# Decay attention and two MLPs on one core: one shape for the score and value matmuls, an order that counts shape changes, six P buffers

## Chip, cores and metric

One core of a Trainium2 chip runs the whole program in one launch. The metric is the device time of the launch in microseconds; lower is better.

## What is computed

Attention with a causal mask and a decay over 4 batches of 8 heads, 576 positions, 64 channels a head; its output, as 2304 tokens of 512 channels, goes through two MLPs (512 to 2048 to 512) with different activations.

```python
scores = scale * np.matmul(q, k.transpose(0, 1, 3, 2))
cum = np.cumsum(np.log(np.clip(f, 0.0001, 1.0)), axis=-1)
decay = cum[:, :, :, None] - cum[:, :, None, :]
scores = np.where(causal, -1000000000.0, scores + decay)
attn = np.exp(scores - np.max(scores, axis=-1, keepdims=True))
attn = attn / (np.sum(attn, axis=-1, keepdims=True) + 1e-09)
attn_out = np.matmul(attn, v)
...
h = x @ w_in; g = np.where(h >= 1, h, np.where(h <= -1, 0.0, (h + 1) ** 2 / 4)); x = g @ w_out
...
h = x @ w_in2; P = a0 + a1*h + a2*h2 + a3*h3; Q = 1 + abs(b0)*abs(h) + abs(b1)*h2; out = (P / (Q + 1e-6)) @ w_out2
```

## The kernel before

**Attention.** Two heads make a pair (16 pairs); head 0 lies on partitions 0 to 63, head 1 on 64 to 127. Each operand of an fp32 product is split into a high and a low part, so a product is three matmuls. A pair's queries are cut into nine blocks (`BLOCKS`): first the last 64 queries of both heads together (the block that the code calls `both`), then the blocks of 128 queries from the last to the first, each for head 0 and head 1. The tasks of a pair (`tasks_of_pair`) are, in the names that the order lists print:

- S, scores in PSUM (L414; L405 for the joint block). For a block of 128 queries the two heads run as pairs of matmuls on partitions 0 to 63 and 64 to 127, which the trace shows starting together: ql by kh, qh by kl, qh by kh, and last the decay, `one` by `ct` ("c"), which reads 2 partitions a head. So TensorE sees a tile of 64 rows three times and then one of 32 rows (2 are used). The joint block uses all 128 rows.
- M (L436, VectorE) adds the mask, takes the row's extreme and writes P; E (L448, ScalarE) is the exponential.
- T (L460) transposes P through TensorE, 128 keys at a time; the last keys are 64, so that piece fills 64 partitions. C (L473, L475, by way of `copy`, L329 on ScalarE and L331 on VectorE) copies T out of PSUM to PT.
- V (L500) multiplies PT with v into O; each head gives 64 columns, so the tile is 128 rows by 64 columns, and 64 by 64 for the last keys. R1 to R6 are the row sums' reciprocals; rT (L528) transposes them, 9 columns.

PSUM has four banks for S, two for T and two for O. `PB` is 5: P has five buffers.

**What fills TensorE beside it.** Weights come in as 64-bit words and are converted (L92 to L112, on ScalarE and VectorE), then split (L126, L130). Of the first MLP's first two chunks of 512 tokens, the products with the first four of the sixteen weight groups (h, L683, and a, L764) are spread through the attention as soon as the pairs that they need are done. After the attention come the rest of both MLPs: h (L683) and a (L777, L779).

**The order.** `plan` makes it: each task has a key (its wanted place), engines that may run it with a stated duration, tasks it needs, and buffers that it takes and frees. It goes through the ready tasks and takes the one with the least of "when it can start, by the stated durations" plus `wk` times its key:

```python
cand = (choice[1] + wk * key, key, n, choice[1], choice[2])
```

Of tasks with two engines it also picks the engine. The list so made is emitted once and then stands: on the chip every engine works through its list in order and waits at semaphores, whatever the stated durations were. The MLP part is planned by a second call.

Of the kernel before, what the change touches and what calls it, by code (L numbers as in the profile page):

```python
# [7 lines left out]
F32 = mybir.dt.float32  # L8
# [4 lines left out]
ALU = mybir.AluOpType  # L13
# [5 lines left out]
def kernel(ctx, tc, qT, kT, v, f, w_in1, w_out1, w_in2, w_out2, a, b, out):  # L19
# [24 lines left out]
    CM, CE = 80, 144  # L44
    PB = 5
    FILL = 2
    SB, TB_, OB, RB = 4, 2, 2, 2
    KM, KEX, KT, KC, KV, KR, KX, PKL, LK, FE, FS = 0.0, 1.0, 2.0, 2.0, 4.0, 2.0, 9.0, 5.0, 12.0, 170.0, 40.0
    I_K, I_Q = 4.4, 5.2
    CS = 12.0  # L50
    WARM, WARM2 = 12, 14
    WK = 0.003

# [127 lines left out]
    qd = [[ap1.tile([P, P], F32R, name=f"qd{y}{n}") for y in "hl"] for n in range(2)]  # L181
    ct = [ap1.tile([P, S], F32R, name=f"ct{n}") for n in range(2)]
    one, oned = [ap1.tile([P, P], F32R, name=f"one{x}") for x in range(2)]
    half = ap1.tile([P, 2], F32, name="half")
# [17 lines left out]
    def load_pair(pr, x):  # L202
        if x < 2:
            t = ap2.tile([P, S], F32, tag=("ks", "qs")[x], name=f"{'kq'[x]}s{pr}")
            SP.dma_start(t[:], (kT, qT)[x][pr])
        else:
            t = ap2.tile([P, NC, P], F32, tag="vn", name=f"vn{pr}")
            SP.dma_start(
                t[:, 0:NC - 1, :], v[pr, 0:(NC - 1) * P, :].rearrange("(c p) d -> p c d", p=P)
            )  # L210
            SP.dma_start(t[0:QB, NC - 1, :], v[pr, (NC - 1) * P:S, :])
        nat[pr, x] = t
# [22 lines left out]
    def task(key, eng, dur, fn, deps=(), take=(), free=()):  # L235
# [3 lines left out]
        return len(tasks) - 1  # L239

    done, by = {}, {}
    clock = dict.fromkeys(LAT, T0)
    clock["sp"] = 3.0
# [4 lines left out]
    def plan(first, wk):  # L248
# [10 lines left out]
        while ready:  # L259
            best = None  # L260
            for n in ready:
                key, ways, deps, take, _ = tasks[n]
                free_at = 0.0
                ok = True
                need = {}
                for tag in take:
                    k = need[tag] = need.get(tag, 0) + 1
                    if len(bufs[tag]) < k:
                        ok = False
                        break  # L270
                    free_at = max(free_at, sorted(bufs[tag])[k - 1])
                if not ok:
                    continue
                choice = None
                for w, (eng, dur, _) in enumerate(ways):
                    at = max(clock[eng], free_at)
                    for d in deps:
                        e2 = by[d]
                        at = max(at, done[d] + (0.13 if e2 == eng and eng != "pe" else 0.0 if e2 == eng else LAT[e2]))
                    end = at + dur if len(ways) > 1 else 0.0  # L280
                    if choice is None or end < choice[0]:
                        choice = (end, at, w)

                cand = (choice[1] + wk * key, key, n, choice[1], choice[2])
                if best is None or cand < best:
                    best = cand
# [8 lines left out]
            if eng == "sp":  # L295
                for issue, moved in dur:
                    dma[0] = max(dma[0], at) + issue
                    dma[1] = max(dma[1], dma[0] + 0.64) + MOVE * moved
                clock[eng] = dma[0]
                done[n] = dma[1] + LAND  # L300
            elif eng == "init":
                done[n] = dur
            else:
                clock[eng] = at + dur
                done[n] = at + dur
# [33 lines left out]
    def tasks_of_pair(pr):  # L339
# [48 lines left out]
        for pos, (b, j) in enumerate(BLOCKS):  # L388
# [8 lines left out]
            def s_fn(s=s, b=b, both=both, cuts=cuts):  # L397
# [13 lines left out]
                for x, (qq, kk_) in enumerate(((ql_, kh), (qh, kl_), (qh, kh), (one, c_))):  # L411
                    for jj in range(2):
                        pp = slice(jj * QB, jj * QB + (QB if x < 3 else 2))
                        PE.matmul(  # L414
                            ts[jj][:, 0:n], qq[pp, qc] if x < 3 else qq[pp, :], kk_[pp, 0:n], start=(x == 0), stop=(x == 3)
                        )
# [3 lines left out]
            if j == 1:  # L420
                tid[pr, f"S{pos}"] = tid[pr, f"S{pos - 1}"]
            else:
                dur = 4 * sum(mm(n1 - n0) for n0, n1 in cuts) if both else 4 * max(mm(w), 0.22)
                T(f"S{pos}", s, "pe", 0.08 + dur, s_fn, ("klo", "ldc", "qlo", "qd0", "qd1", prev), ("S", "S"),
                  ("k", "q") if pos == NB - 2 else ())

            def max_fn(s=s, w=w, pos=pos, both=both):
# [25 lines left out]
            for c0, c1 in [(0, LAST), (LAST, NC)] if both else [(0, b + 1)]:  # L453
                rows = QB if c0 == LAST else P

                def t_fn(s=s, c0=c0, c1=c1, rows=rows):
                    p = Pt[s]
                    ps = Tt[s, c0] = psT.tile([P, 512], F32, tag="T", name=f"T{s}_{c0}")
                    for c in range(c0, c1):
                        PE.transpose(  # L460
                            ps[0:rows, (c - c0) * P:(c - c0 + 1) * P], p[:, c * P:c * P + rows], ident[:]
                        )

                T(f"T{pos}_{c0}", s + KT, "pe", 0.107 * (c1 - c0), t_fn, (f"E{pos}",),
                  ("T",), ("P",) if c1 == b + 1 else ())

                def c_fn(eng, s=s, g=g, j=j, qo=qo, c0=c0, c1=c1, rows=rows, both=both):
                    if (pr, g) not in PT:
# [3 lines left out]
                    if both:  # L472
                        copy(eng, to[0:rows, c0:c1, :, qo:qo + QB], src[0:rows, 0:n].rearrange("p (c j x) -> p c j x", j=2, x=QB))  # L473
                    else:
                        copy(eng, to[0:rows, c0:c1, j, qo:qo + P], src[0:rows, 0:n].rearrange("p (c x) -> p c x", x=P))  # L475

# [7 lines left out]
        for g in (1, 0):  # L484
# [5 lines left out]
            for c in range(ncs):  # L490
                c_q = max(0, c * P - q0)
                rows = QB if c == LAST else P

                def pv_fn(g=g, c=c, c_q=c_q, rows=rows, n=n, ncs=ncs):
                    if c == 0:
                        Ot[pr, g] = psO.tile([P, 512], F32, tag="O", name=f"O{pr}_{g}")
                    o, pt = Ot[pr, g], PT[pr, g]
                    for j in range(2):
                        pp = slice(j * D, (j + 1) * D)
                        PE.matmul(  # L500
                            o[pp, c_q:n], nat[pr, 2][0:rows, c, pp], pt[0:rows, c, j, c_q:n],
                            start=(c == 0), stop=(c == ncs - 1),
# [3 lines left out]

                T(f"V{g}{c}", s0 + last + KV, "pe", mm(n - c_q, 4) + 0.06, pv_fn,
                  deps + ["ldv"] + ([f"V{g}{c - 1}"] if c else []) + (["V14"] if g == 0 else []), ("O",) if c == 0 else (),
                  ((f"PT{g}",) + (("v",) if g == 0 else ())) if c == ncs - 1 else ())

            def o_fn(eng, g=g, q0=q0, n=n):
# [9 lines left out]
        def r1():  # L521
            r = Rt[pr] = ap2.tile([P, NB], F32, tag="r", name=f"r{pr}")
            DVE.tensor_scalar(out=r[:], in0=ls[pr][:], scalar1=1e-9, scalar2=None, op0=ALU.add)
            DVE.reciprocal(r[:], r[:])

        def r2():
            Rr[pr] = psT.tile([P, 512], F32, tag="T", name=f"rT{pr}")
            PE.transpose(Rr[pr][0:NB, 0:P], Rt[pr][:], ident[:])  # L528

# [562 lines left out]
```

## Time and profile before

| | us |
|---|---|
| three runs | 1020.82, 1021.68, 1025.32; median 1021.68 |
| the profiled execution | 1021.83 |
| its span, first to last instruction | 1020.0 |
| TensorE (PE) busy | 1003.8 (98%) |
| VectorE (DVE), ScalarE (ACT), GpSimd (POOL) busy | 739.6, 631.9, 377.0 |

Matmul records carry modelled ends, and they overlap, so a busy PE says little of what it costs. The distance from one matmul's start to the next one's start is what a matmul takes when nothing is waited for, and it is read from the timeline.

### The profile page before, as it was taken

What the parts mean: (1) busy time and instruction counts of PE and PEld (TensorE: products, weight loads), DVE (VectorE), ACT (ScalarE), POOL (GpSimd) and SP (SyncE); (2) the same over time, 40 slices, a digit from 0 to 9 for tenths busy, and PEclk for the clock granted to TensorE, in tenths of its full rate; (3) what the DMA queues carried; (4) which work ended last, traced back from release to release, by engine and by line L of the source; (5) the groups of instructions that cost most, each with busy time, mean ns of one, the idle gap of its engine ahead of it and who ended that gap; (6) DMA issues with size and microseconds to landing.
All of it is one profiled execution on the core that took longest, in us unless ns stands there. A gap on an engine that the chain in (4) does not pass through costs nothing.

```text
span 1020.0 us, 15449 instructions
## 1 busy us (share of the span) xinstructions
PE 1003.8 (98%) x5274; PEld 796.4 (78%) x5274; DVE 739.6 (73%) x1411; ACT 631.9 (62%) x1312; POOL 377.0 (37%) x331
## 2 busy tenths in 40 slices
PE   8999999999999999999999999999999999999998
PEld 4665666666767888888888998888888888888887
DVE  6888997867287798786874577967667667657646
ACT  5787777767455443433432468876677667666666
POOL 3223320122365532222222133545454444445344
PEclk7999999999999999999999999999999999999999
DMA  5455766622456347565561454001101000010010
GB/s 187 152 176 172 220 204 204 190 67 69 158 189 227 118 152 238 161 205 166 156 225 63 131 179 125 1 10 33 42 0 42 8 35 16 6 42 1 1 42 21
DMA packets 62790, 113.13 MB, mean 111 GB/s; under 512 B 9452, under 2 KB 20348, under 8 KB 62712
## 3 DMA queue, kind: packets, MB, share of 16 engines
q1 hardware_dynamic: 62712, 112.15, 34.5%
q8 instruction: 42, 0.69, 0.3%
q14 instruction: 36, 0.29, 0.1%
HBM read 82.00 MB, written 30.11 MB: 110 GB/s over the span
## 4 chain that ended last, share of the span: by engine, by line
PE 89%; DVE 4%; ACT 2%; issue 2%; DMA 1%; POOL 1%; SPq 1%; ACTq 0%; DVEq 0%
PE h L683 35%; PE a L779 18%; PE a L777 16%; PE S L414 6%; PE T L460 5%; PE O L500 5%; PE a L764 2%; PE S L405 1%; DVE xl L672 1%; POOL wl L130 1%; ACT P L448 0%; DMA xr<-xd 0%; ACT PT L329 0%; DMA qs<-in_q_dram 0%; PE rT L528 0%
## 5 line engine op out<-in xcount | busy, mean ns | idle before, releaser
L697 POOL TENSOR_TENSOR gl<-t,gh 128x512 fp32r<-128x512 f32 (+1 forms) x160 | 195.7, 1224 | 323.3 <-ACT gh L693 238.9
L683 PE MATMUL h<-xl,wh 128*128 128x512 f32 (+1 forms) x640 | 236.5, 370 | 2.4 <-DVE xl L672 2.1
L683 PE MATMUL h<-xh,wl 128*128 128x512 f32 (+1 forms) x640 | 237.2, 371 | 1.0 <-ACT xh L668 1.0
L683 PE MATMUL h<-xh,wh 128*128 128x512 f32 (+1 forms) x640 | 235.6, 368 | 0.0
L693 ACT CAST gh<-t 128x512 fp32r<-128x512 f32 (+1 forms) x160 | 93.0, 582 | 112.7 <-PE a L779 47.8
L728 POOL TENSOR_TENSOR t<-t,t 128x512 f32<-128x512 f32 (+1 forms) x80 | 94.5, 1181 | 126.8 <-ACT t L721 123.4
L683 PEld LDWEIGHTS h<-xl,wh 128*128 128x128 f32 x640 | 120.7, 189 | 25.1 <-DVE xl L672 5.8
L683 PEld LDWEIGHTS h<-xh,wl 128*128 128x128 f32 x640 | 120.7, 189 | 22.3 <-ACT xh L668 1.4
L683 PEld LDWEIGHTS h<-xh,wh 128*128 128x128 f32 x640 | 120.7, 189 | 19.9
L779 PE MATMUL a<-wh,gl 128*128 128x512 f32 x288 | 112.3, 390 | 0.0
L779 PE MATMUL a<-wl,gh 128*128 128x512 f32 x288 | 112.2, 390 | 0.0
L779 PE MATMUL a<-wh,gh 128*128 128x512 f32 x288 | 112.1, 389 | 0.0
L777 PE MATMUL a<-gl,wh 128*128 128x512 f32 (+1 forms) x288 | 105.3, 366 | 0.0
L777 PE MATMUL a<-gh,wl 128*128 128x512 f32 (+1 forms) x288 | 105.3, 366 | 0.0
L777 PE MATMUL a<-gh,wh 128*128 128x512 f32 (+1 forms) x288 | 105.3, 365 | 0.0
L707 ACT ACTIVATE t<-t 128x512 f32<-128x512 f32 (+1 forms) x80 | 47.1, 589 | 91.6 <-DVE t L702 91.3
L746 DVE SCALAR_TENSOR_TENSOR t<-t,na,h 128x512 f32<-128x512 f32 (+1 forms) x80 | 55.4, 692 | 57.2 <-ACT h L742 56.1
L448 ACT ACTIVATE P<-P,nm 128x576 f32<-128x576 f32 (+2 forms) x144 | 83.7, 584 | 19.1 <-DVE nm L436 16.9
L702 DVE TENSOR_SCALAR t<-h 128x512 f32<-128x512 f32 (+1 forms) x80 | 50.7, 633 | 58.5 <-PE h L683 58.4
L732 DVE TENSOR_TENSOR t<-h,t 128x512 f32<-128x512 f32 (+1 forms) x80 | 51.0, 637 | 48.8 <-ACT t L724 48.5
L436 DVE CUSTOM_DVE_ANT_0 P<-S,tri 128x256 f32<-128x256 f32 (+1 forms) x144 | 66.9, 477 | 17.1 <-PE S L414 15.8
L718 ACT ACTIVATE t<-h,ab 128x512 f32<-128x512 f32 (+1 forms) x80 | 51.9, 651 | 41.9 <-PE h L683 41.7
(115 smaller groups left out, 1905.5 us busy)
## 6 DMA issues: line engine op xcount, KB each, us to landing
raw<-in_moe_w_in_dram SPq DMA_DIRECT2D x32, 512.0 KB
raw<-in_moe_w_out_dram SPq DMA_DIRECT2D x32, 512.0 KB
xr<-xd SPq DMA_DIRECT2D x48, 256.0 KB
wfd<-wd SPq DMA_DIRECT2D x44, 256.0 KB
wf<-wfd SPq DMA_DIRECT2D x44, 256.0 KB
ks<-in_k_dram SPq DMA_DIRECT2D x16, 288.0 KB
qs<-in_q_dram SPq DMA_DIRECT2D x16, 288.0 KB
xd<-xa SPq DMA_DIRECT2D x16, 288.0 KB
```

What stands on the lines that cost most here:

```text
L414: PE.matmul(ts[jj][:, 0:n], qq[pp, qc] if x < 3 else qq[pp, :], kk_[pp, 0:n], start=(x == 0), stop=(x == 3))
L436: DVE.tensor_tensor_reduce(out=p[:, n0:n1], in0=t[:, 0:n1 - n0], in1=m, scale=-1.0 / ROOT, scalar=least, op0=ALU.add, op1=ALU.min, accum_o ...
L448: ACT.activation(p, p, AF.Exp, scale=-1.0, bias=nm[pr][:, pos:pos + 1], accum_out=ls[pr][:, COL[pos]:COL[pos] + 1])
L460: PE.transpose(ps[0:rows, (c - c0) * P:(c - c0 + 1) * P], p[:, c * P:c * P + rows], ident[:])
L683: PE.matmul(hps[g], ww[:, kk * P:(kk + 1) * P], xx[kk], start=(kk == 0 and y == 0), stop=(kk == KD - 1 and y == 2))
L693: ACT.copy(gt[g][0], mid[g][0])
L697: eng.tensor_tensor(out=lo, in0=mid.pop(g)[0], in1=hi.bitcast(F32), op=ALU.subtract)
L718: ACT.activation(mid[g]["w"], hps[g], AF.Abs, scale=ab[:, 0:1])
L728: POOL.tensor_tensor(out=vv, in0=vv, in1=mid[g]["w"], op=ALU.add)
L746: DVE.scalar_tensor_tensor(out=t, in0=t, scalar=na[:, 0:1], in1=hps[g], op0=ALU.add, op1=ALU.mult)
L777: PE.matmul(acc[x, d], ww[:, dd], gg, start=st, stop=sp)
L779: PE.matmul(acc[x, d], gg[:, dd], ww[:], start=st, stop=sp)
```

## The change

Four things are changed together.

1. c's matmul reads 64 partitions a head (`ct` and `one` were zero and one there already), so all four matmul pairs of S have a tile of 64 rows by 128 columns.
2. The last keys are handled as a full piece of 128: T takes keys 448 to 575, v's last piece lies on partitions 64 to 127 of a tile whose first 64 are zero (`vt`, two tiles made once, set to zero by GpSimd at the start), and V's last product has 128 rows. rT transposes 128 columns (`rt_`) where it had 9.
3. `plan` keeps the last shape at TensorE. S tasks carry "rows", V tasks "columns", all others none. A TensorE task of another shape than the last gets `SWC` added when candidates are compared, and `SWT` to its duration. The keys' offsets `KT`, `KC`, `KV` grow (T, C and V are wanted two or three blocks later), `WK` grows, loads lead by more (`LK`, `PKL`), and the stated durations of S and V are changed.
4. P has six buffers.

```diff
-    PB = 5
+    PB = 6
-    KM, KEX, KT, KC, KV, KR, KX, PKL, LK, FE, FS = 0.0, 1.0, 2.0, 2.0, 4.0, 2.0, 9.0, 5.0, 12.0, 170.0, 40.0
+    KM, KEX, KT, KC, KV, KR, KX, PKL, LK, FE, FS = 0.0, 1.0, 4.0, 4.0, 7.0, 2.0, 9.0, 7.0, 14.0, 170.0, 40.0
-    WK = 0.003
+    WK = 0.025
+    SWC, SWT = 0.1, 0.19
...
+    vt = [ap1.tile([P, NC, P], F32, name=f"vt{n}") for n in range(2)]
+    rt_ = [ap1.tile([P, P], F32, name=f"rt{n}") for n in range(2)]
+    for n in range(2):
+        POOL.memset(vt[n][0:QB, NC - 1, :], 0.0)
+        POOL.memset(rt_[n][:], 0.0)
...
-            SP.dma_start(t[0:QB, NC - 1, :], v[pr, (NC - 1) * P:S, :])
+            SP.dma_start(t[QB:P, NC - 1, :], v[pr, (NC - 1) * P:S, :])
...
-                cand = (choice[1] + wk * key, key, n, choice[1], choice[2])
+                turn = SWC if ways[0][0] == "pe" and shape.get(n) != at_shape[0] else 0.0
+                cand = (choice[1] + turn + wk * key, key, n, choice[1], choice[2])
...
+                if eng == "pe" and shape.get(n) != at_shape[0]:
+                    at_shape[0] = shape.get(n)
+                    dur += SWT
...
-                        pp = slice(jj * QB, jj * QB + (QB if x < 3 else 2))
+                        pp = slice(jj * QB, (jj + 1) * QB)
...
-                dur = 4 * sum(mm(n1 - n0) for n0, n1 in cuts) if both else 4 * max(mm(w), 0.22)
-                T(f"S{pos}", s, "pe", 0.08 + dur, s_fn, ("klo", "ldc", "qlo", "qd0", "qd1", prev), ("S", "S"),
+                dur = 4 * sum(mm(n1 - n0) for n0, n1 in cuts) if both else 4 * max(mm(w), 0.12)
+                T(f"S{pos}", s, "pe", 0.02 + dur, s_fn, ("klo", "ldc", "qlo", "qd0", "qd1", prev), ("S", "S"),
...
+                if not both:
+                    shape[tid[pr, f"S{pos}"]] = "rows"
...
-                        PE.transpose(
-                            ps[0:rows, (c - c0) * P:(c - c0 + 1) * P], p[:, c * P:c * P + rows], ident[:]
-                        )
+                        k0 = min(c * P, S - P)
+                        PE.transpose(ps[:, (c - c0) * P:(c - c0 + 1) * P], p[:, k0:k0 + P], ident[:])
...
-                            o[pp, c_q:n], nat[pr, 2][0:rows, c, pp], pt[0:rows, c, j, c_q:n],
+                            o[pp, c_q:n], nat[pr, 2][:, c, pp], pt[:, c, j, c_q:n],
...
-                T(f"V{g}{c}", s0 + last + KV, "pe", mm(n - c_q, 4) + 0.06, pv_fn,
+                T(f"V{g}{c}", s0 + last + KV, "pe", mm(n - c_q, 4) + 0.03, pv_fn,
...
+                shape[tid[pr, f"V{g}{c}"]] = "columns"
...
-            PE.transpose(Rr[pr][0:NB, 0:P], Rt[pr][:], ident[:])
+            PE.transpose(Rr[pr][:, 0:P], rt_[pr % 2][:], ident[:])
```

New lines move the numbers: what was L414, L460, L500, L528, L436, L331 is L430, L478, L515, L544, L454, L347.

**TensorE's list in the third pair (pr = 2), before**, from the end of the 512-wide S to the start of the 384-wide one. S_0_618 and S_0_619 are the two heads; O_0 is the product for the first 256 queries; T_4 is the last keys.

```order
L414 MATMUL S_0_618<-ct_127,one_129 128x512
L414 MATMUL S_0_619<-ct_127,one_129 128x512
L528 MATMUL rT_631<-ident,r_601 9x128
L460 MATMUL T_0_633<-ident,P_596 128x128 x4
L500 MATMUL O_0_647<-PT_0_582,vn_179 64x256 x2
L460 MATMUL T_4_654<-ident,P_596 64x128
L500 MATMUL O_0_647<-PT_0_582,vn_179 64x128 x2
L414 MATMUL S_0_661<-kh_115,ql_120 128x384
```

**The same pair in the change**, from the end of the 256-wide S to the start of the 128-wide one.

```order
L430 MATMUL S_0_651<-ct_127,one_137 128x256
L430 MATMUL S_0_652<-ct_127,one_137 128x256
L478 MATMUL T_4_664<-ident,P_574 128x128
L478 MATMUL T_0_666<-ident,P_597 128x128 x4
L515 MATMUL O_0_674<-PT_0_570,vt_130 64x256 x2
L515 MATMUL O_0_674<-PT_0_570,vt_130 64x128 x2
L478 MATMUL T_0_688<-ident,P_604 128x128 x4
L478 MATMUL T_0_698<-ident,P_661 128x128 x3
L430 MATMUL S_0_704<-kh_115,ql_120 128x128
```

The two pieces of O_0 now stand side by side with no transposition between, the transpositions of three blocks stand around them, and the 256-wide S follows the 384-wide one directly.

**VectorE's list in that pair, before**, from the maximum of the first 512-wide block (the rows with nm alone read out its result).

```order
L436 ISA P_638,nm_594<-S_0_618,tri 128x512
L436 ISA nm_594 128x1
L331 COPY PT_1_650<-T_0_633 128x8x64
L436 ISA P_659,nm_594<-S_0_619,tri 128x512
L436 ISA nm_594 128x1
L96 TENSOR_SCALAR wd<-wd 128x512
L100 TENSOR_SCALAR wd<-wd 128x512
L436 ISA P_696,nm_594<-S_0_661,tri 128x384
```

**And in the change.**

```order
L454 ISA P_597,nm_572<-S_0_560,tri 128x512
L454 ISA nm_572 128x1
L347 COPY PT_0_570<-T_0_581 128x128
L454 ISA P_604,nm_572<-S_0_561,tri 128x512
L454 ISA nm_572 128x1
L382 TENSOR_TENSOR ql_122<-qs_268,qh_121 128x576
L385 TENSOR_TENSOR qdl_126<-ql_122,half 128x128
L347 COPY xa_624<-O_1_593 128x320
```

The 512-wide copy of the joint block's T has left VectorE here (ScalarE has it now), a 128-wide one of the pair before stands in its place, and a copy of O has come to it.

## Rows read from the trace of the kernel before

**Rows 1.** The page: span, and busy time of each engine.
```profile
span 1020.0 us, 15449 instructions
PE 1003.8 (98%) x5274; PEld 796.4 (78%) x5274; DVE 739.6 (73%) x1411; ACT 631.9 (62%) x1312; POOL 377.0 (37%) x331
```

**Rows 2.** Windows: busy us by engine in five stretches, TensorE's granted clock, DMA.
```profile
core 0: us, PE busy (x) PEld busy (x) DVE busy (x) ACT busy (x) POOL busy (x), PEclk, DMA share, GB/s
12.00:30.00 18.00, 17.61 (x76) 10.46 (x76) 11.65 (x38) 10.57 (x31) 1.66 (x2) 0.55 0.44 145
30.00:90.00 60.00, 56.92 (x423) 36.56 (x421) 53.00 (x161) 48.27 (x138) 19.19 (x15) 0.97 0.53 163
90.00:140.00 50.00, 48.80 (x337) 33.27 (x336) 47.83 (x121) 37.75 (x102) 15.98 (x14) 1.00 0.66 202
140.00:260.00 120.00, 120.00 (x841) 81.41 (x841) 88.76 (x261) 85.80 (x243) 20.86 (x20) 1.00 0.42 137
310.00:1020.00 710.00, 705.72 (x3377) 594.11 (x3375) 501.47 (x784) 416.43 (x745) 282.73 (x236) 1.00 0.27 87
```

**Rows 3.** What PE waited for from 12 to 140 us.
```profile
PE S L405 <- DMA ct<-ft: 2.9, 1, 2.9
PE T L460 <- ACT P L448: 2.1, 4, 0.8
```

**Rows 4.** Timeline of PE, third pair: start us, us, instruction; then the next pair's.
```profile
43.49 0.50 PE L414 MATMUL S<-kh,ql 64*128 64x512 f32 x2
43.83 0.39 PE L414 MATMUL S<-kl,qh 64*128 64x512 f32 x2
44.06 0.39 PE L414 MATMUL S<-kh,qh 64*128 64x512 f32 x2
44.38 0.50 PE L414 MATMUL S<-ct,one 2*128 2x512 f32 x2
44.81 0.28 PE L528 MATMUL rT<-ident,r 128*9 128x128 f32 x1
...
50.15 0.33 PE L414 MATMUL S<-kh,ql 64*128 64x128 f32 x2
50.32 0.27 PE L414 MATMUL S<-kl,qh 64*128 64x128 f32 x2
50.43 0.28 PE L414 MATMUL S<-kh,qh 64*128 64x128 f32 x2
50.63 0.33 PE L414 MATMUL S<-ct,one 2*128 2x128 f32 x2
...
56.21 0.50 PE L414 MATMUL S<-kh,ql 64*128 64x512 f32 x2
```

**Rows 5.** Timeline of PE: h, and a transposition into 9 columns behind it.
```profile
105.06 0.39 PE L683 MATMUL h<-xl,wh 128*128 128x512 f32 x1
105.30 0.39 PE L683 MATMUL h<-xh,wh 128*128 128x512 f32 x1
105.52 0.27 PE L528 MATMUL rT<-ident,r 128*9 128x128 f32 x1
```

**Rows 6.** Groups of DVE from 30 to 140 us: busy us, mean ns | idle before.
```profile
L331 DVE COPY PT<-T 128x512 f32<-128x512 f32 x10 | 6.7, 688 | 0.6 <-PE T L460 0.5
...
L366 DVE TENSOR_TENSOR kl<-ks,kh 128x576 fp32r<-128x576 f32 x5 | 4.9, 987 | 0.1
L366 DVE TENSOR_TENSOR ql<-qs,qh 128x576 fp32r<-128x576 f32 x6 | 4.6, 767 | 0.3 <-ACT qh L362 0.3
```

**Rows 7.** Timeline of PE in the first pair.
```profile
13.80 0.63 PE L414 MATMUL S<-kl,qh 64*128 64x512 f32 x2
14.22 0.63 PE L414 MATMUL S<-kh,qh 64*128 64x512 f32 x2
```

**Rows 8.** Timeline of PE after the attention: h of the fourth chunk, with its waits.
```profile
288.83 0.50 PE L683 MATMUL h<-xl,wh 128*128 128x512 f32 x1 [1.09 <-DVE xl L672]
...
291.95 0.50 PE L683 MATMUL h<-xh,wl 128*128 128x512 f32 x1 [1.01 <-ACT xh L668]
```

More of the change, by code (lines that the diff above doesn't have):

```diff
@@ L206, in load_pair @@
         else:
-            t = ap2.tile([P, NC, P], F32, tag="vn", name=f"vn{pr}")
+            t = vt[pr % 2]
             SP.dma_start(
@@ L239, in task @@
         return len(tasks) - 1
+    shape = {}
     done, by = {}, {}
+    at_shape = [None]
     clock = dict.fromkeys(LAT, T0)
@@ L453, in tasks_of_pair, with t_fn @@
             for c0, c1 in [(0, LAST), (LAST, NC)] if both else [(0, b + 1)]:
-                rows = QB if c0 == LAST else P
-                def t_fn(s=s, c0=c0, c1=c1, rows=rows):
+                def t_fn(s=s, c0=c0, c1=c1):
                     p = Pt[s]
@@ L459, in t_fn, with c_fn @@
                     for c in range(c0, c1):
-                        PE.transpose(
-                            ps[0:rows, (c - c0) * P:(c - c0 + 1) * P], p[:, c * P:c * P + rows], ident[:]
-                        )
+                        k0 = min(c * P, S - P)
+                        PE.transpose(ps[:, (c - c0) * P:(c - c0 + 1) * P], p[:, k0:k0 + P], ident[:])
                 T(f"T{pos}_{c0}", s + KT, "pe", 0.107 * (c1 - c0), t_fn, (f"E{pos}",),
                   ("T",), ("P",) if c1 == b + 1 else ())
-                def c_fn(eng, s=s, g=g, j=j, qo=qo, c0=c0, c1=c1, rows=rows, both=both):
+                def c_fn(eng, s=s, g=g, j=j, qo=qo, c0=c0, c1=c1, both=both):
                     if (pr, g) not in PT:
@@ L472, in c_fn @@
                     if both:
-                        copy(eng, to[0:rows, c0:c1, :, qo:qo + QB], src[0:rows, 0:n].rearrange("p (c j x) -> p c j x", j=2, x=QB))
+                        copy(eng, to[:, c0:c1, :, qo:qo + QB], src[:, 0:n].rearrange("p (c j x) -> p c j x", j=2, x=QB))
                     else:
-                        copy(eng, to[0:rows, c0:c1, j, qo:qo + P], src[0:rows, 0:n].rearrange("p (c x) -> p c x", x=P))
+                        copy(eng, to[:, c0:c1, j, qo:qo + P], src[:, 0:n].rearrange("p (c x) -> p c x", x=P))
                 engs = ["act", "dve"]
@@ L491, in tasks_of_pair, with pv_fn @@
                 c_q = max(0, c * P - q0)
-                rows = QB if c == LAST else P
-                def pv_fn(g=g, c=c, c_q=c_q, rows=rows, n=n, ncs=ncs):
+                def pv_fn(g=g, c=c, c_q=c_q, n=n, ncs=ncs):
                     if c == 0:
@@ L521, in r1 @@
         def r1():
-            r = Rt[pr] = ap2.tile([P, NB], F32, tag="r", name=f"r{pr}")
-            DVE.tensor_scalar(out=r[:], in0=ls[pr][:], scalar1=1e-9, scalar2=None, op0=ALU.add)
-            DVE.reciprocal(r[:], r[:])
+            r = rt_[pr % 2][:, 0:NB]
+            DVE.tensor_scalar(out=r, in0=ls[pr][:], scalar1=1e-9, scalar2=None, op0=ALU.add)
+            DVE.reciprocal(r, r)
         def r2():
             Rr[pr] = psT.tile([P, 512], F32, tag="T", name=f"rT{pr}")
-            PE.transpose(Rr[pr][0:NB, 0:P], Rt[pr][:], ident[:])
+            PE.transpose(Rr[pr][:, 0:P], rt_[pr % 2][:], ident[:])
         def r3():
```

## The prediction, made before the changed kernel was run

> **What bounds the kernel now.** I read the page first, then the stretches, then TensorE's timeline. The page gives TensorE 98% of a span of 1020.0 us [rows 1]; since ends are modelled, that only says where to look. The stretches [rows 2] show two regimes. From 310 us on, in the MLPs, TensorE's records leave 4 us of 710 open; nothing that the change touches runs there, and that part will stay. Before it, in the attention, TensorE is as full (56.9 of 60, 48.8 of 50, 120.0 of 120 us), but VectorE is nearly so too, up to 140 us: 53.0 of 60 and 47.8 of 50, then 88.8 of 120. TensorE's waits from 12 to 140 us are few: 2.9 us for c's first load, 2.1 us for exponentials [rows 3]. So in the attention TensorE sets the time, with VectorE close behind in the first half.
>
> The question is then what a matmul costs there, and the timeline tells it [rows 4]. A pair of 512-wide matmuls, both heads at once, takes 0.23 us when the next pair has the same shape (43.83 to 44.06). The first pair after a transposition takes 0.34, the last before c takes 0.32, and c itself 0.43. So a change of tile shape costs about 0.10 us in the matmul ahead of it and 0.10 in the one behind it, and c, between two changes, pays both. In 128-wide matmuls the same places read 0.17, 0.11 and 0.20: 0.06 behind a change, 0.09 ahead of one. A change is therefore worth 0.15 us beside narrow work (I price transpositions and V like it) and 0.20 beside wide matmuls.
>
> **What counts as a change.** A transposition into 9 columns shows none: h to h takes 0.24 us, h to rT 0.22 [rows 5]. So in counting TensorE's list I take transpositions, whatever their width, as full tiles, which gives 288 changes before and 108 after, 180 fewer. The Trainium skill, TensorEngine Tiling (Array Packing), Key Properties, says that changing the tiling mode drains TensorE; S agrees, the 9-column rows do not. By that rule the narrow transpositions would count as well, 302 before, and 14 more at 0.15 us would make the gain 2 us larger.
>
> **The sum, part by part.**
>
> 1. c on 64 rows removes 64 changes, one in each group of S. In a 512-wide group, qh goes from 0.32 to 0.23 and c from 0.43 to 0.33, as it still leaves the shape: 0.19 us. I take that for 384 and 256 too, and 0.15 for 128: 0.72 us a pair, times 16 is **11.5 us**. The additional rows cost nothing: qh by kh has 64 rows and takes 0.23.
> 2. Full last keys remove 16 changes in V at 0.15 us: **2.4 us**. The transposition and the copy have the same width, 128 columns, as before; only the partitions double. For the transpositions into 64 and 9 columns I expect nothing (above).
> 3. The order removes the other 100. Their surroundings are mixed, so 0.17 us each: **17 us**. The lists show how: both pieces of O_0 side by side, two S in a row.
>
> Together **31 us** less for TensorE, 1.9 us a pair. If every change cost 0.145 it would be 26 us, at 0.20 it would be 36. No record of before shows a change from 64 rows straight to 128; between those two ends it must lie, since both kinds of neighbours are there.
>
> 4. What is given back to VectorE. The third pair takes 12.72 us from its 512-wide S to the next one's [rows 4]; without 1.94 us that is 10.78. VectorE is busy 88% of the time there [rows 2], 11.2 us a pair. Its list gets shorter: counted over the attention, it loses four kl and two ql to GpSimd (0.99 and 0.77 us) and 15 copies of T to ScalarE (0.69 us for a 512-wide one [rows 6], narrower ones less, 7 us in all), and gains two copies of O and two small ones; about 10.7 us in all, 0.67 a pair. That leaves 10.6 us of work in a pair of 10.8, which two engines that wait for each other won't keep. The densest stretch of before has VectorE at 47.83 of 50, 96% [rows 2]: at that share a pair takes 11.0 us, 0.26 more than TensorE's; at the 88% of the early stretch 12.0, 1.2 more. Over the ten pairs up to some 140 us this gives back 2.6 to 11.9 us. I take **6**, nearer the lower end, because the 96% was reached while TensorE was 98% busy. After that VectorE has 26% free and I take nothing.
> 5. ScalarE gets those copies: 48.3 of 60 us busy early; in 15% less time that is 95% of it. It is off the path as long as it stays under VectorE; this is in the upper end of item 4.
> 6. The way into the MLPs. In the list, 95 wide matmuls stand between the last V and the first h of the fourth chunk before, 84 now, but eight others have moved behind the last rT instead; the net is three fewer, at 0.23 us each 0.7 us less to cover a chain (reciprocals, the last store, loading and splitting x) that was already late by 1.09 and 1.01 us [rows 8]. I take **1 us** more waiting, 0 to 3 as bounds.
> 7. Four more memsets on GpSimd before its first product: TensorE waits 2.9 us for c's load at that time [rows 3], and I take zero; uncovered, it would be under 1 us. On SP's queue the number of transfers is the same and v's last piece only lands on other partitions; larger leads issue k and q earlier. Zero. The sixth P buffer and the later keys for T let TensorE pass a late exponential; at most the 2.1 us of those waits [rows 3].
>
> Sum: -31 + 6 + 1 = -24. Against the profiled execution's own 1021.83 us (median of the runs 1021.68, so no correction) that is **998 us**. All ends together run from 988 (36 less, 2.6 back) to 1011 (26 less, 11.9 and 3 back).
>
> **The rivals.**
>
> - *VectorE and ScalarE take over in the first half.* The in-order lists then keep only the 88% of the early stretch, all 11.9 us come back, and the transition costs 3: about 1006 us. For it: 53.0 of 60 us already, and moved work lands on ScalarE, itself 80% busy. Against it: 96% was held for 50 us. 20%.
> - *The buffers and the wider spacing also take out the waits.* From 30 to 140 us TensorE's records leave 4.3 us open [rows 2]; without these and with nothing given back: 986 us. For it, the waits on the exponential name that place; against it, VectorE's share. 11%.
> - *c's cost isn't its shape.* Its matmul reads `ct` and `one`, which no other does; if the 0.43 us came from there, 11.5 us stay and it ends at 1009 us. Against it: the matmul behind any change, T to S, is longer by the same 0.1. 4%.
> - *Slower, by the clock.* From 12 to 30 us the granted clock is 0.55, near the lower level of 1.2 GHz, after TensorE had waited 2.9 us for c, and a 512-wide pair takes 0.42 us there against 0.23 [rows 2, 3, 7, 4]. It came back at 2.4 GHz, but dipped once more up to 90 us (0.97). That stretch is in both kernels. But if a TensorE that now waits for VectorE in every pair stays at 1.2 GHz beyond 30 us, each microsecond of full-clock work costs 0.83 us more (0.42 over 0.23): the 31 us are gone after 37 us of such work, three and a half pairs, and beyond 43 us, four pairs, it is slower by over 0.5%. Were it so for five pairs, 54 us of work, the time would be 1021.8 + 45 - 31 + 1 = 1037 us (what VectorE takes back hides in it). Against it: the clock was full through 90 to 140 with 2.4% open. 3%. The Trainium skill, TensorE: Matmul & The Clock Gate, Part 1, has the clock throttled by default and released by activity; both rows agree with that direction.
>
> **Chances.** The forecast, 991 to 1003, has 58%; the rivals 20, 11, 4 and 3, in their order; 4% are left for no change, the gain eaten by waits that I don't see. Half a percent, about 5 us, is what a measurement of this kernel can tell from no change. Faster by more: 58 + 20 + 11 + 4 = 93%; within it 4%; slower 3%. For 8 in 10 the range takes the forecast and most of the two nearest rivals, one on either side: 987 to 1009.
>
> **What would show it.** In the profile after: the matmul of c 0.23 us behind the one before it and 0.33 ahead of a transposition in 512-wide groups; the third pair in 11.0 to 12.0 us instead of 12.72; VectorE at 92 to 97% up to about 130 us; the end of the attention about 25 us earlier, and the MLPs behind it as long as before. I'm wrong if TensorE's list shows gaps of over 0.5 us in most pairs, if the granted clock falls between 30 and 230 us for more than a few microseconds, or if h and a wait much longer than 5 us in all at the transition.

## The result, and the profile after

The changed kernel took 988.76 us, the median of four runs (988.53 to 989.36), where the kernel before took 1023.5 on the same chip (1020.82 to 1026.03): a ratio of 0.9662, with an interval of 0.9631 to 0.9692. The prediction was 998 us. The profiled execution took 988.63 us, so its span, 986.9 us, is the one to set against the 1020.0 of [rows 1]; it is 33.1 us shorter:

```profile
span 986.9 us, 15400 instructions
...
PE 970.6 (98%) x5274; PEld 793.0 (80%) x5274; DVE 733.3 (74%) x1394; ACT 631.3 (64%) x1325; POOL 387.6 (39%) x339
```

TensorE has the same 5274 matmuls and the same 98%; what went is time inside its list. The stretches, with the columns of [rows 2]:

```profile
12.00:30.00 18.00, 16.03 (x138) 11.84 (x137) 17.09 (x54) 15.32 (x48) 3.08 (x3) 1.00 0.64 204
30.00:90.00 60.00, 57.47 (x461) 42.62 (x460) 57.66 (x177) 53.82 (x158) 23.88 (x20) 1.00 0.60 193
90.00:130.00 40.00, 39.47 (x304) 29.94 (x302) 37.69 (x100) 33.51 (x93) 16.14 (x14) 1.00 0.60 187
130.00:235.00 105.00, 102.98 (x795) 78.91 (x794) 80.45 (x230) 81.60 (x234) 26.09 (x21) 1.00 0.53 173
285.00:987.00 702.00, 697.66 (x3342) 587.38 (x3340) 496.58 (x775) 412.16 (x738) 280.32 (x233) 1.00 0.28 86
```

VectorE is at 96% and 94% up to 130 us (57.66 of 60, 37.69 of 40), as forecast. The MLPs leave 4.3 us open, as before. The surprise stands in the first row: 138 matmuls where 76 were, and a granted clock of 1.00 where it was 0.55. TensorE's timeline shows how the first pair begins, where the third begins, and what the shapes did in the fourth:

```profile
9.02 0.31 PE L421 MATMUL S<-kh,qdh 128*128 128x320 f32 x1
9.97 0.38 PE L421 MATMUL S<-ct,one 66*128 66x320 f32 x1 [0.64 <-DMA ct<-ft]
...
31.59 0.53 PE L430 MATMUL S<-kh,ql 64*128 64x512 f32 x2
...
43.29 0.50 PE L430 MATMUL S<-kh,ql 64*128 64x512 f32 x2
43.62 0.39 PE L430 MATMUL S<-kl,qh 64*128 64x512 f32 x2
43.85 0.39 PE L430 MATMUL S<-kh,qh 64*128 64x512 f32 x2
44.09 0.40 PE L430 MATMUL S<-ct,one 64*128 64x512 f32 x2
44.41 0.44 PE L478 MATMUL T<-ident,P 128*128 128x128 f32 x2
...
48.15 0.33 PE L430 MATMUL S<-kh,qh 64*128 64x384 f32 x2
48.32 0.34 PE L430 MATMUL S<-ct,one 64*128 64x384 f32 x2
48.49 0.28 PE L430 MATMUL S<-kh,ql 64*128 64x256 f32 x2
...
55.28 0.50 PE L430 MATMUL S<-kh,ql 64*128 64x512 f32 x2
```

c starts 0.24 us behind qh, and the transposition 0.32 behind c: in [rows 4] the same places read 0.32 and 0.43. Further down the 256-wide S follows the 384-wide c after 0.17 us, the same distance as from qh to c ahead of it (48.15 to 48.32): no change is paid there. The third pair takes 11.70 us from its 512-wide S to the next one's (31.59 to 43.29), where it took 12.72, and the fourth 11.99 (to 55.28). The last products with v begin at 226.17 us, 30.9 us earlier than before (257.10); some 25 were forecast.

TensorE's waits, in us in total, times and the longest, up to 300 us:

```profile
PE T L478 <- DVE PT L347: 2.8, 4, 1.1
PE h L699 <- DVE xl L688: 2.6, 4, 1.5
PE T L478 <- ACT PT L345: 2.2, 5, 0.6
...
PE S L421 <- DMA ct<-ft: 0.6, 1, 0.6
```

The 2.9 us for c's load [rows 3] are 0.6. The waits on exponentials no longer stand at the head of the list, and waits for the copies of T have come.

**Where the 33.1 us went.** For each run I added up TensorE's matmuls at the plain distance of their kind, plus 0.10 us on either side of a shape change (0.05 behind narrow work): "list" below. What the trace has beyond this is waiting and lower clock, divided into the start (to 30 us), the attention (to the last V) and the transition to the fourth chunk's h. About 1.2 us lie in the MLPs, in every run but a_dve and a_dve_pb8 (0.1). The four columns leave 6 to 7 us of every span: this, and what lies ahead of the first matmul and behind the last. The sums are mine; the spans are the trace's. The list holds the forecast's own prices, so it tests the number of changes and not what one costs; that is read from the timelines, at b_c64 below. Its level depends on the plain distances: the medians of all these traces put some 5 us more into every list and as much less into every attention, so the differences between runs are firmer than the columns.

| run | span | changes | list | start | attention | transition |
|---|---|---|---|---|---|---|
| before | 1020.0 | 288 | 984.7 | 11.8 | 11.6 | 4.8 |
| after | 986.9 | 108 | 953.6 | 5.5 | 16.2 | 4.5 |
| b_c64 | 1006.7 | 222 | 972.4 | 8.7 | 13.5 | 5.0 |
| a_c2 | 995.7 | 199 | 970.3 | 4.4 | 9.2 | 4.5 |
| b_start | 1020.1 | 288 | 984.7 | 11.9 | 11.2 | 4.9 |
| b_warm | 1016.6 | 288 | 987.5 | 7.6 | 9.3 | 5.0 |
| b_wk | 1004.8 | 281 | 984.1 | 2.3 | 6.3 | 5.0 |
| a_wk | 1010.0 | 124 | 956.8 | 7.3 | 26.1 | 12.9 |
| b_order | 995.4 | 220 | 973.5 | 3.5 | 6.8 | 4.5 |
| a_nocount | 996.3 | 187 | 967.8 | 3.3 | 13.1 | 4.9 |
| a_pb5 | 989.9 | 110 | 953.9 | 5.6 | 20.5 | 2.9 |
| a_pool | 989.2 | 109 | 954.0 | 4.6 | 20.2 | 3.4 |
| a_dve | 985.9 | 118 | 955.6 | 3.5 | 16.3 | 4.5 |
| a_dve_pb8 | 985.6 | 121 | 956.5 | 3.5 | 15.0 | 4.6 |

From before to after: list 31.1 us less, start 6.3 less, attention 4.6 more, transition 0.3 less. The forecast had 31, nothing, 6 and 1 more. Of the changed kernel's 16.2 us the profile names 4.7 as waits (30 to 235 us): a short wait lies under the modelled end of the matmul ahead of it and shows only as a longer distance.

Each row is one execution, and the start varies. In 19 executions of the kernel before, the mean granted clock ran from 0.985 to 0.993, and the two ends took 1026.37 and 1018.2 us: how long the clock stays low differs from one execution to the next. Differences of the start by a few microseconds between runs with that stretch (before, b_c64, b_start, b_warm, a_wk) need not be due to the edit.

### The profile page after: what moved, and what is told of

Its sections match the earlier page's. It is cut to its first block, busy times and chain, and to the rows that moved or that the text cites. A ratio compares the mean times of both kernels' runs of the same rounds, so it can differ in the third digit from the quotient of the medians.

```text
span 986.9 us, 15400 instructions
## 1 busy us (share of the span) xinstructions
PE 970.6 (98%) x5274; PEld 793.0 (80%) x5274; DVE 733.3 (74%) x1394; ACT 631.3 (64%) x1325; POOL 387.6 (39%) x339
## 4 chain that ended last, share of the span: by engine, by line
PE 81%; DVE 10%; ACT 3%; issue 3%; DMA 1%; POOL 1%; SPq 0%; POOLq 0%; DVEq 0%; ACTq 0%
PE h L699 36%; PE a L795 19%; PE a L793 16%; PE T L478 3%; PE O L515 2%; PE S L430 2%; DVE P L454 2%; DVE xl L688 1%; ACT P L466 1%; PE a L780 1%; DVE wd L97 1%; PE S L421 1%; POOL wl L131 1%; DVE PT L347 1%; DVE wd L107 1%
## 5 line engine op out<-in xcount | busy, mean ns | idle before, releaser
L699 PEld LDWEIGHTS h<-xh,wl 128*128 128x128 f32 x640 | 120.7, 189 | 20.5 <-ACT xh L684 0.7
L478 PE MATMUL T<-ident,P 128*128 128x128 f32 x400 | 63.9, 281 | 5.8 <-DVE PT L347 2.8
```

The costliest lines, as they stand in the source:

```text
L478: PE.transpose(ps[:, (c - c0) * P:(c - c0 + 1) * P], p[:, k0:k0 + P], ident[:])
L699: PE.matmul(hps[g], ww[:, kk * P:(kk + 1) * P], xx[kk], start=(kk == 0 and y == 0), stop=(kk == KD - 1 and y == 2))
```

## The experiments

Names that begin with b_ are edits of the kernel before, with a_ of the changed one. Ratios are to the kernel before on the same chip. The kernel before itself varied, from 1018.2 to 1026.37 us in 19 runs of one comparison, and so did b_start (1020.95 to 1027.64) and b_warm (1014.73 to 1023.11); the others by less than 4 us.

**c's shape alone**, in the kernel before (b_c64), and taken back in the changed one (a_c2).

```diff
-                        pp = slice(jj * QB, jj * QB + (QB if x < 3 else 2))
+                        pp = slice(jj * QB, (jj + 1) * QB)
```

> The kernel before with c's matmul on 64 rows and every list as it was. Theory 1 (each change of shape costs TensorE 0.10 us on either side, and TensorE sets the time): 64 changes fewer, 0.72 us a pair, 11.5 us less in all, some 1011 us; c's matmul 0.23 us behind the one before it in 512-wide groups. Theory 2 (VectorE takes most of it back in the first ten pairs): 4 to 7 us less. Theory 3 (c's cost is its operands, not its shape): no change.

> The changed kernel with c's matmul back on 2 rows, lists as in the change. Theory 1: 64 changes more, 11.5 us more, some 1000 us. Theory 2 (with the start mended and six buffers, VectorE has become the bound and TensorE has room): 3 to 7 us more.

b_c64 took 1008.87 us, 0.9874 (0.9838 to 0.991). Its third pair, with the same lists and the same operands as in [rows 4]:

```profile
39.39 0.40 PE L414 MATMUL S<-kh,qh 64*128 64x512 f32 x2
39.62 0.39 PE L414 MATMUL S<-ct,one 64*128 64x512 f32 x2
39.95 0.28 PE L528 MATMUL rT<-ident,r 128*9 128x128 f32 x1
```

The distance from qh to c is 0.23 us and from c to rT 0.33, where [rows 4] have 0.32 and 0.43. By the medians of both timelines, the two together are shorter by 0.19 us in 512, 384 and 256-wide groups and by 0.14 in 128-wide ones, as item 1 priced them. So the price of a change stands, and the rival that c's cost comes from its operands falls. The span is 13.3 us shorter, and the list 12.3 for 66 changes, against the 11.5 that I had put down for 64 (twice one S follows another, and c's change went on both sides). The rest isn't shape: the start is 3.1 us better, with the clock at 0.91 from 12 to 30 us instead of 0.55, and the attention waits 1.9 us more. a_c2 took 996.87 us, 0.9755 (0.9719 to 0.979), 8 us more than the changed kernel. That lies between the two theories. Its list grew by 16.7 us, more than in b_c64, because S now often follows S: c on 2 rows puts a change on both its sides there, 91 in all. Half of these 16.7 us came out of waits that went (attention 16.2 to 9.2). Under the change's order half of what the shape saves is given back.

**The start.** Why did c come early enough? b_start moves c's parts ahead of k's cast, and c's load on SP ahead of the third pair's k and the first raw weights; everything else keeps its order. b_warm instead puts twelve more matmuls in front, to keep TensorE busy until c is there.

```diff
+    chain = range(first_c, tid[0, "c"] + 1)
+    moved = [o for o in order_ if o[0] in chain]
+    at_k = next(k for k, (n, _) in enumerate(order_) if n == tid[0, "khi"])
...
+    order_ = [o for o in order_[:at_c + 1] if o not in sp_late] + sp_late + order_[at_c + 1:]
...
-    task(-99, "pe", 0.22 * WARM2, lambda: warm(WARM2), (t,), ("T",), ("T",))
+    task(-99, "pe", 0.22 * WARM2, lambda: warm(WARM2 + 12), (t,), ("T",), ("T",))
```

> The kernel before with the first microseconds in the order of the changed kernel and all else as it was: c's two parts are made ahead of the casts of k and q, and c's load stands ahead of a load of k and one of raw weights on SP's queue. Theory 1 (the late load of c costs its wait and, behind it, 17 us at half clock): wait for c under 1 us, granted clock 1.0 from 12 to 30 us, 5 to 7 us less. Theory 2 (VectorE bounds the first pairs anyway): the wait goes, the time falls by 0 to 2 us.

> The kernel before with 12 more of the matmuls on zeros that stand ahead of the first score, lists as they were: TensorE is at work while c's load is under way. Theory 1: c lands as before, so S starts no earlier, but the clock stays at 2.4 GHz, and the cold stretch's cost goes, 4 to 6 us less. Theory 2 (first pairs bound by VectorE): the clock stays up, 0 to 2 us less. If the clock falls all the same: no change.

b_start: 1021.71 us, 1.0009 (0.9986 to 1.0032), no change. c came in time and the wait reappeared one step on, at VectorE, which is Theory 2's side. TensorE's wait, VectorE's timeline behind it, and the stretch from 12 to 30 us:

```profile
PE S L414 <- DVE nm L436: 3.0, 1, 3.0
```

```profile
10.12 0.30 DVE L369 TENSOR_TENSOR qdl<-ql,half 128x128 fp32r<-128x128 f32 x1
14.02 0.43 DVE L96 TENSOR_SCALAR wd<-wd 128x512 f32<-128x512 f32 x1 [3.60 <-ACT wd L92]
14.48 0.43 DVE L100 TENSOR_SCALAR wd<-wd 128x512 int32<-128x512 int32 x1
14.82 0.42 DVE L436 CUSTOM_DVE_ANT_0 P<-S,tri 128x256 f32<-128x256 f32 x1
```

```profile
12.00:30.00 18.00, 14.34 (x65) 8.49 (x63) 11.81 (x38) 10.97 (x31) 1.66 (x2) 0.62 0.48 175
```

VectorE stood 3.60 us for a weight conversion that its list has ahead of the first maximum (L436); the scores behind it couldn't leave PSUM, and the clock fell as before. b_warm: 1018.9 us, 0.9969 (0.9945 to 0.9993). There is no wait for c, and yet the clock fell, later: in the profiled execution the stretch at the lower level was 6.8 us instead of 17.1. The twelve matmuls cost 2.9 us of list, the start's loss fell by 4.2 (11.8 to 7.6) and the attention's by 2.3. Its ten executions run from 1014.73 us at a mean clock of 0.999 to 1023.11 at 0.989. So the clock is part of it, but twelve matmuls aren't the cure.

**WK alone.** Both point to the order of the lists in the first pairs, and the change has one constant for that, the weight that a task's key has against the time at which it can start.

```diff
-    WK = 0.003
+    WK = 0.025
```

> The kernel before with WK = 0.025 alone: the planner weighs the keys more, so that c's parts and load come first and the first weights' conversion stands behind the first pair's maxima on VectorE and ScalarE; 281 changes of shape against 288. Theory 1 (the start was bound twice, by c's late load and by conversions ahead of the first maxima; without both the clock stays up): TensorE's waits up to 30 us fall from 11.8 to about 5.5 us, 5 to 7 us less in all, some 1015 us. Theory 2 (the first pairs lose elsewhere what they gain): within 2 us of before.

> The change with the weight of the keys as before (WK = 0.003), all else as in the change; 124 changes of shape, 3 us of TensorE's time more than in the change. Theory 1 (the larger WK keeps weight conversions and other work that isn't due from standing ahead of the scores' chain on VectorE and ScalarE; that gave the start 6 us and the rest of the attention some 5): 8 to 16 us more than the change, with TensorE's waits up to 30 us back near 12 us. Theory 2 (with shapes and six buffers in place WK no longer matters): 3 us more.

b_wk, the kernel before with this constant alone: 1006.97 us, 0.9841 (0.9817 to 0.9866), 15.2 us of span, with 281 changes and the list 0.6 us shorter. Start 9.5 less, attention 5.3 less; in all, two to three times the 5 to 7 us of Theory 1. SP's list of before, then of the changed kernel; b_wk has c's load at 6.03 and the raw weights at 11.37:

```profile
6.31 0.43 SPq L82 DMA_DIRECT2D raw<-in_moe_w_in_dram  x1
6.85 2.48 SPq L220 DMA_DIRECT2D ct<-ft  x4
```

```profile
6.07 2.48 SPq L228 DMA_DIRECT2D ct<-ft  x4
...
11.41 0.42 SPq L83 DMA_DIRECT2D raw<-in_moe_w_in_dram  x1
```

VectorE in the kernel before, and its first maximum in b_wk:

```profile
11.64 0.43 DVE L96 TENSOR_SCALAR wd<-wd 128x512 f32<-128x512 f32 x1 [1.58 <-ACT wd L92]
12.10 0.43 DVE L100 TENSOR_SCALAR wd<-wd 128x512 int32<-128x512 int32 x1
13.31 0.42 DVE L436 CUSTOM_DVE_ANT_0 P<-S,tri 128x256 f32<-128x256 f32 x1 [0.78 <-PE S L405]
```

```profile
10.83 0.42 DVE L436 CUSTOM_DVE_ANT_0 P<-S,tri 128x256 f32<-128x256 f32 x1 [0.50 <-PE S L405]
```

With the larger weight, work that is not yet due no longer slips ahead because it happens to be ready. The stretches of b_wk show the rest:

```profile
12.00:30.00 18.00, 18.00 (x145) 12.56 (x144) 16.73 (x52) 16.55 (x51) 4.47 (x5) 1.00 0.67 220
30.00:90.00 60.00, 58.59 (x435) 38.23 (x434) 56.22 (x166) 50.81 (x142) 27.58 (x23) 1.00 0.58 180
90.00:140.00 50.00, 49.33 (x344) 33.99 (x344) 42.87 (x115) 37.25 (x104) 15.16 (x15) 1.00 0.55 176
```

The clock never falls. VectorE has 42.87 us of work in the 50 where it had 47.83 [rows 2], but 56.22 in the 60 ahead of them where it had 53.00: the work lies earlier, and TensorE is fuller in both stretches (58.59 for 56.92, 49.33 for 48.80). Of the attention's 5.3 us the clock holds some 1.5, by my estimate: in the kernel before it fell for another 3.4 us at 86 us (the 0.97 in [rows 2]), and 0.23 us of work took 0.42 at that level [rows 4, 7]. a_wk is the changed kernel with 0.003: 1010.8 us, 0.9888 (0.9859 to 0.9917), 22 us more than with 0.025, where Theory 1 had 8 to 16; with 124 changes. Its waits, up to 300 us:

```profile
PE h L699 <- ACT xh L684: 6.0, 2, 4.3
PE T L478 <- ACT PT L345: 4.4, 7, 1.3
PE T L478 <- DVE PT L347: 4.3, 4, 2.6
PE S L421 <- DMA ct<-ft: 2.5, 1, 2.5
```

c's load is late again and the clock is 0.91 from 12 to 30 us. In the transition the 4.3 us wait is followed by matmuls at the lower clock, until 285 us; both are in its 12.9 us. Without the new WK the other parts are worth 10 us of span (1020.0 to 1010.0), with it 17.9 (1004.8 to 986.9).

**The order without the shapes** (b_order: c on 2 rows, last keys on 64, rT from 9 columns), **and the shapes without the count** (a_nocount).

```diff
-    SWC, SWT = 0.1, 0.19
+    SWC, SWT = 0.0, 0.0
```

> The change without its shapes: planner, keys, WK and six P buffers as in the change, but c on 2 rows, last keys as 64, rT of 9 columns. Its list has 220 changes of shape (before 288, the change 108). Theory 1: 68 changes fewer are 11 us, the start 6 us, and 3 to 5 come back to VectorE: 1007 to 1011 us. Theory 2 (order and buffers work by hiding waits, not by changes of shape): TensorE's waits between 30 us and the last V fall from 11 us to under 6, and the time to under 1003 us.

> The change with SWC = SWT = 0: the planner doesn't count shape changes, all else as in the change. Its list has 187 changes against 108, 14 us of TensorE's time by the prices of the timeline. Theory 1 (TensorE sets the time, but VectorE stands close behind, so that about half of what TensorE saves comes back): 7 to 12 us more than the change, 996 to 1001 us. Theory 2 (TensorE alone): 14 us more. Theory 3 (the other keys do it): under 3 us more.

b_order: 996.84 us, 0.9743 (0.9719 to 0.9767), nearer to Theory 2: the attention's waits fell to 6.8 us, where it had under 6. Its list is 19.9 us longer than the changed kernel's, its waits 11.4 shorter: the three shapes are worth 8.5 us of span where their list says 20. a_nocount: 996.88 us, 0.9741 (0.9712 to 0.9771), as its Theory 1 said: the count saves 79 changes and 14.2 us of list, and 9.4 us of span (8.1 by the medians).

b_order also bears on what VectorE's share does. Its stretch from 30 to 90 us:

```profile
30.00:90.00 60.00, 59.71 (x453) 40.69 (x452) 57.07 (x174) 53.08 (x155) 23.37 (x19) 1.00 0.59 188
```

VectorE is busy 57.07 of the 60 us, 95%, about as in the changed kernel, and TensorE leaves 0.29 us open, where the changed kernel leaves 2.53.

**Buffers and VectorE.** If VectorE's load is what gives back, an idler VectorE takes waits out. a_pool puts kl, ql and the two diagonal products of all pairs from the third on GpSimd; a_dve raises the duration that `cost` states for a VectorE operation, so that the plan gives it less (the attention's weight conversions, stated elsewhere, keep theirs). a_pb5 takes the sixth buffer back; a_dve_pb8 adds two to a_dve.

```diff
-        ways = ["dve", "pool"]
+        ways = ["dve", "pool"] if pr < 2 else ["pool"]
...
-            return 0.07 + (0.52e-3 if kind == "ts" else 1.04e-3) * n
+            return 0.15 + (0.52e-3 if kind == "ts" else 1.04e-3) * n
...
-    PB = 6
+    PB = 5
...
-    PB = 6
+    PB = 8
```

> The change with the low parts of k and q and the two diagonal products on GpSimd alone from the third pair on: VectorE has 9.7 us less up to the seventh pair and 8.6 us less in the next nine (by the mean durations of before), GpSimd some 25 us more. Theory 1 (VectorE is what gives TensorE its 16 us of waits in the attention): these waits fall by 5 to 10 us and so does the time, to 979 to 984 us. Theory 2 (the waits are the lists' latencies, not VectorE's load): within 2 us of the change. Theory 3 (GpSimd's work slows VectorE, or its products come late): 2 us or more above the change.

> The change with VectorE's stated durations 0.08 us longer each, as its records are (0.68 and 0.08 us for a 512-wide maximum that was stated as 0.62): the planner moves copies to ScalarE and products to GpSimd, VectorE's list is shorter by 7.8 us up to the seventh pair and by 6.1 us in the next nine, ScalarE's longer by 2.8 and 5.3 us; 118 changes of shape, 2 us more of TensorE's time. Theory 1 (VectorE's load): 2 to 6 us less than the change. Theory 2 (latencies): 2 us more, from the changes of shape. Theory 3 (ScalarE becomes the bound): 2 us more or above.

> The change with five P buffers; its list has 110 changes against 108. Theory 1 (the sixth buffer only gives the planner room): 0 to 3 us more than the change. Theory 2 (the sixth buffer is what keeps TensorE's waits at 16 us while it works 31 us less): 4 us more or above.

> The change with VectorE's stated durations 0.08 us longer, as in a_dve, and eight P buffers in place of six; 121 changes of shape, 1 us more of TensorE's time than a_dve. Theory 1 (TensorE's waits in the attention come from P buffers that are held until their transposition, as five against six cost 3 us): waits between 30 us and the last V fall from 16 to 10 to 13 us, and the time to 981 to 985 us. Theory 2 (six buffers suffice; what waits is left is the chain of maximum, exponential, transposition and copy through two full engines): within 2 us of a_dve, 985 to 989 us.

a_pool: 991.08 us, 0.9691 (0.9659 to 0.9722). Its stretches from 30 to 90 and 90 to 130 us:

```profile
30.00:90.00 60.00, 56.35 (x443) 41.22 (x442) 49.31 (x153) 52.84 (x154) 32.41 (x31) 0.97 0.57 184
90.00:130.00 40.00, 37.84 (x292) 29.67 (x291) 34.84 (x91) 32.10 (x91) 23.26 (x19) 1.00 0.61 187
```

VectorE has 8 us less in the first (49.31 for 57.66) and 3 in the second, and yet the attention's waits rose from 16.2 to 20.2 us. The time is 2.3 us more, as Theory 3 had it. Some operations that stayed on VectorE became slower meanwhile; one group from 30 to 130 us, in a_pool and in the changed kernel:

```profile
L113 DVE SCALAR_TENSOR_TENSOR wd<-raw,wd 128x512 int32<-128x512 int32 x8 | 8.0, 997 | 0.1
```

```profile
L113 DVE SCALAR_TENSOR_TENSOR wd<-raw,wd 128x512 int32<-128x512 int32 x10 | 7.0, 702 | 0.1
```

These means hold few operations: L107, of the same kind, has 853 ns in a_pool and 848 in the changed kernel, and b_wk has 1040 for the same conversion (its L112) without any move to GpSimd. Single operations in a_pool show what happens:

```profile
63.90 0.68 DVE L107 SCALAR_TENSOR_TENSOR wd<-raw,wd 128x512 int32<-128x512 int32 x1
...
64.70 1.92 DVE L113 SCALAR_TENSOR_TENSOR wd<-raw,wd 128x512 int32<-128x512 int32 x1
```

```profile
64.64 1.43 POOL L382 TENSOR_TENSOR kl<-ks,kh 128x576 fp32r<-128x576 f32 x1 [1.96 <-ACT kh L378]
```

The conversion takes 0.68 us with GpSimd idle, and 1.92 where GpSimd's kl runs beside it for 1.37 us.

a_dve: 986.61 us (985.17 to 987.65), 0.9649 (0.9623 to 0.9675). The same two stretches:

```profile
30.00:90.00 60.00, 57.27 (x448) 42.65 (x445) 52.87 (x161) 54.44 (x160) 29.59 (x26) 0.97 0.58 185
90.00:130.00 40.00, 39.95 (x314) 31.21 (x314) 34.38 (x93) 34.05 (x96) 17.00 (x13) 1.00 0.62 191
```

VectorE has 88% and 86%, and the attention waits 16.3 us, as before the edit. VectorE's share, on which my item 4 was built, does not set these waits by itself: b_order waits little with 95%, a_dve as long with less. All four runs of a_dve lie below the changed kernel's four, in Theory 1's range of time but not by its mechanism: the start lost 2.0 us less, the list grew by 2.0, and the 1.0 us that the span lost lies in the MLPs, whose plan has the new durations too. It is the best version with a_dve_pb8 (987.18 us, 0.9656, 0.9637 to 0.9674), but the intervals of the ratios, measured on different chips, overlap the changed kernel's: not clearly different. a_pb5: 991.63 us, 0.969 (0.9665 to 0.9716). The sixth buffer is worth 3 us (attention waits 20.5 against 16.2, part of it regained in the transition); a seventh and eighth, nothing.

## Why the prediction was right and wrong

- **The time.** 988.76 us lies in the range of 987 to 1009, but below the 991 to 1003 of the forecast itself, 9 us under its 998. Of these 9 us the start holds 6.3, the attention 1.4 and the transition 1.3. The range reached so low for the second rival's sake, whose mechanism did not come; that the time lies in it is partly luck.
- **Items 1 to 3, the list: right.** 31 us forecast, 31.1 by the list, with the 180 changes counted beforehand. As the list is made with the same prices, the proof of them is b_c64's timeline, with 0.19 us a wide group. How it divides was less so. In b_order the order without the shapes has 68 fewer changes and 11.2 us, where item 3 had 100 and 17; the shapes add 19.9, where items 1 and 2 had 13.9, since only with c on 64 rows can one S follow another without a change.
- **Item 7 failed.** "On SP's queue the number of transfers is the same" and "larger leads issue k and q earlier. Zero", and in the rival on the clock: "That stretch is in both kernels." The number is the same, the order is not: c's load now stands ahead of the first raw weights. And the stretch at 0.55 is gone, with 6.3 us of the start. The diff had the constant responsible, WK, and no step priced it; in the kernel before it alone brings 15.2 us, nearly half of the gain.
- **Item 4 hit its number by a sum of two misses.** Against before the attention waits 4.6 us more, near the 6. But WK alone took 5.3 out, and against b_wk the rest of the change put 9.9 back, beside 3.2 at the start: 17.9 us came of a list 30.5 shorter. Nor did they come where item 4 put them. From 30 to 130 us TensorE's records leave 3.06 us open, where before left 4.28 from 30 to 140 [rows 2]; from 130 to 235 they leave 2.02, where before left none from 140 to 260. There VectorE is 77% busy, and item 4 had "I take nothing". The third pair's 11.70 us were within its "11.0 to 12.0". The reason given, VectorE's share, was there (96%) and does not explain the waits: b_order had 95% and waited 6.8 us, and two runs with VectorE at 82 to 88% waited as long as the changed kernel or longer.
- **Item 6: +1 forecast, -0.3 found**; the bounds of 0 to 3 just miss it. a_wk shows that the transition can cost far more (12.9 us, part of it at the lower clock) when the list puts its work late.
- **The buffers.** "At most the 2.1 us" was too little by a microsecond for the sixth buffer alone: without it the attention's waits are 4.3 us longer, and 1.6 of that is regained in the transition.
- **The rivals.** The number of the second, 986 us, is the nearest to the result, but not by its mechanism: buffers and spacing did not take the attention's waits out, the start and WK made up for them. The clock did matter, with the sign that no rival had: in the kernel before it fell during a wait of 2.93 us and stayed at the lower level for 17.1 us; in the changed kernel, with a wait of 0.64 us in that place, it stayed up. The Trainium skill, TensorE: Matmul & The Clock Gate, Part 1, has activity release the clock; the two kernels agree in direction.

**What stays open.** Some 16 us of waits, by the sums of the table, remain in the changed kernel's attention. In three comparisons they follow the list: what shortened it by 14 to 20 us gave back a third to more than half (a_nocount, a_c2, b_order to after). VectorE's share alone does not explain them, and eight P buffers in a_dve took 1.3 us of them and no time. The chain from maximum over exponential, transposition and copy, whose links stand in four in-order lists, would fit the names in the waits; none of the runs tried it by itself, and which link sets the pace is not shown.

## What to carry to other kernels

Count shape changes in TensorE's list and price one from the timeline, where the same matmul stands with and without it: the price that one timeline gave held in b_c64's. But where a planner makes in-order lists, price every constant in the diff, the smallest too, and compare the lists of all engines and queues at the start: how readily ready work may pass due work was worth 15 us. And don't take all that a list loses as saved: of the shapes' 17 to 20 us, 8 to 9 reached the span.

## What the runs showed of the hardware that I had not expected

- A short wait at the start can cost more than itself. During the 2.93 us for c's load the clock fell to the lower of its two levels and stayed there for 17.1 us, 16.2 of them behind the wait. With 0.23 us of work in 0.42 [rows 4, 7], my estimate is that some 7.3 of these are lost, and 2.93 and 7.3 make most of the 11.8 us of the start. The length is not a matter of the wait alone: behind 2.5 us for the same load, b_c64 and a_wk had 3.4 us at the lower level, and b_start 13.7 us behind 3.0 for a maximum. With 0.64 us in that place the granted clock stayed at 1.00.
- Work moved from VectorE to GpSimd can come back as longer work on VectorE. In a_pool a VectorE conversion of 128x512 took 0.68 us with GpSimd idle and 1.92 us beside GpSimd's kl. The Trainium skill, SBUF — State Buffer, Who interferes with whom, has a VectorE instruction with two SBUF inputs contend with a GpSimd instruction that reads SBUF. The conversion has two inputs (raw, wd), and these rows agree; what it cost a_pool in all is not shown. GpSimd was busy 55.7 us of the 100 from 30 to 130 us, where the changed kernel has 40.0.
